# Moving the operands of the f32r matrix products to multiples of 256 bytes

## The chip, the core and the metric

The kernel runs on one NeuronCore of a Trainium2 chip. Five engines work side by side: TensorE (PE, with its weight loads shown apart as PEld), VectorE (DVE), ScalarE (ACT), GpSimd (POOL) and SyncE (SP, which only issues DMAs here). The metric is device time in microseconds (us) of one execution; the three runs of the kernel before have a median of 734.86 us (734.58 to 734.96).

On-chip memory (SBUF) has 128 partitions. A tile lies in all of them at the same start address, counted in bytes along the partition. This text gives such an address modulo 512 ("at 192" means that the address leaves 192 when divided by 512).

## The reference

Two attention steps are followed by a gated feed-forward layer, for 8 batches of 576 tokens, 8 heads of 64:

```
def sm_attn(qq, kk, vv):
    s = scale * np.matmul(qq, kk.transpose(0, 1, 3, 2))
    ...
    return np.matmul(a, vv)
p_packed = sm_attn(p, k, v)              # 32 packed queries per head
out = sm_attn(q, p_packed, p_packed)     # 576 queries against 32 packed keys
...
g = x @ w_gate                            # x: 4608 x 512, w_gate, w_val: 512 x 1536
silu = g * (1.0 / (1.0 + np.exp(-g)))
val = x @ w_val
return (silu * val @ w_out).astype(np.float32)
```

## The kernel before

The weights arrive as 64-bit floats and are converted on the chip (lines 192 to 201). For each batch the kernel multiplies the packed values with the two input weight matrices first, which gives a matrix M for the batch (`m_mm`, line 575, products at line 267), and then multiplies the attention weights of the 576 queries (`a2`) with M: this gives the gate and the value (`gv_chunk`, line 619, products at line 633). ScalarE takes the silu, VectorE multiplies, and the result h is multiplied with w_out (`out_mm`, line 650, products at line 652). d_ff is worked through in 12 chunks of 128.

The large products are made in f32r, a faster float32 form of lower precision. To keep the precision each operand is split into a high and a low word (`mh` and `ml` for M, `a2h` and `a2l`, `hh` and `hl`, `wo_h` and `wo_l`), and three products replace one: low by high, high by low, high by high. Of each product one operand is stationary (loaded into the array by an LDWEIGHTS) and one is moving (streamed through it). At line 633 M is stationary (128 columns, 512 bytes of a partition) and a2 is moving (256 or 320 columns); at line 652 h is stationary and w_out is moving (512 columns). Batch 0 makes its products at lines 787 and 828, some of them in plain float32, where one product shows as two MATMUL rows.

The order of the instructions of every engine is written out by hand: `PROGRAM` for batch 0, the tables `FIRST` and `LATER` for the others. Nothing in it is chosen by a planner from addresses or sizes.

Tiles are laid one after another in SBUF in the order in which their names first occur, so a longer tile shifts all that follow it. Three tiles of the kernel before are longer than what they hold: `pp` by `PAD` = 120 elements (480 bytes), `r2` by 52 elements (208 bytes), and `t4` by 48 elements (192 bytes); only the part that is used is ever read. The starts that result, in the built program:

| tile | used as | start modulo 512, before |
|---|---|---|
| w0 to w5 | moving, line 267 | 192 |
| wo_h, wo_l, wo_f | moving, lines 652 and 828 | 192 |
| a2h, a2l | moving, lines 633 and 787 | 192; its second half 448 |
| a2f | moving, line 787 | 160 (a 32-byte multiple) and 416 |
| mh | stationary, line 633 | 0 |
| ml | stationary, line 633 | 448 |
| hh, hl | stationary, line 652 | 448 |
| ppt | stationary, line 267 | 384 |
| k_t, q_t, v_t, st | DMA targets | 192 |

The a2 tile has two halves of 576 elements (2304 bytes), one for each half of the contraction, and a product starts in it at element 0, 256 or 320. So its moving operand starts at 192 as often as at 448. The slices of M and h start at multiples of 512 bytes from their tile's start.

Of the kernel before, what the change touches and what calls it, by code (L numbers as in the profile page):

```python
# [10 lines left out]
F32 = mybir.dt.float32  # L11
# [12 lines left out]
P = 128  # L24
NPAR, NHP = 2, 4
NFC = DF // P
# [9 lines left out]
F64_HI_LEAST = float(np.array(897 << 20, np.int32).view(np.float32))  # L36
F64_HI_MOST = float(np.array(0x47EFFFFF, np.int32).view(np.float32))
SPLIT = 5
PAD = 120
LOW_WORD = -(2.0**-51) * 15 / 16  # L40

PROGRAM = """
# [90 lines left out]
def tile_pack_attention_swiglu(ctx: ExitStack, tc: tile.TileContext, qT, kT, v, vq, pT, wgv, wout, out):  # L133
# [4 lines left out]
    const = ctx.enter_context(tc.tile_pool(name="const", bufs=1))  # L138
    pool = ctx.enter_context(tc.tile_pool(name="pool", bufs=1))
# [9 lines left out]
    minus_two = const.tile([P, 1], F32, name="minus_two")  # L149
    nc.gpsimd.memset(minus_two, -2.0)  # L150

    w_t = [const.tile([P, NHP, 2, 2 * P], F32, name=f"w{k}") for k in range(NFC // 2)]

    def run_all(*gens):
        for g in gens:
# [202 lines left out]
    def s1_scale(b):  # L358
        pp = pool.tile([P, NPAR * D + PAD], F32, tag="pp", bufs=1, name="pp")[:, : NPAR * D].rearrange(
            "p (r d) -> p r d", r=NPAR  # L360
        )
        nc.vector.tensor_tensor(
            pp,
            pps[b][0][:, : NPAR * D].rearrange("p (r d) -> p r d", r=NPAR),
            st1[b][2][:, 2].unsqueeze(2).broadcast_to([P, NPAR, D]),
            op=ALU.mult,
        )
        pps[b].append(pp)
# [236 lines left out]
    t4 = {}  # L605
# [113 lines left out]
    with tc.manual_schedule(engines={mybir.EngineType.PE}):  # L719
# [12 lines left out]
            return rows, [ps_acc.tile([P, 512], F32, tag="acc", name="acc") for _ in range(4)]  # L732

        def t4_of(b):
            t4[b // 2] = pool.tile([P, NFC * P + 48], F32, tag="t4", bufs=1, name="t4")[:, : NFC * P].rearrange(
                "p (f t) -> p f t", f=NFC
            )

        with tc.manual_schedule(
            engines={mybir.EngineType.DVE, mybir.EngineType.Activation, mybir.EngineType.SP}  # L740
# [19 lines left out]
            def narrow(_):  # L760
                wide[0] = False
                t4_of(0)
                for x, y in zip((rows, accs), accs_of(0)):
                    x.extend(y)
# [123 lines left out]
            for word in PROGRAM.split():  # L888
                name = word[: word.index(":") + 1] if ":" in word else word.rstrip("0123456789")
# [14 lines left out]
        def batch(b, behind):  # L904
            if not b % 2:
                t4_of(b)
# [114 lines left out]
```

## Time and profile before

| | |
|---|---|
| median of 3 runs | 734.86 us (734.58 to 734.96) |
| the profiled execution | 734.87 us |
| its span, first to last instruction | 733.1 us |
| TensorE busy / weight loads busy | 723.9 us (99%) / 590.4 us (81%) |
| VectorE busy / ScalarE busy | 454.2 us (62%) / 373.7 us (51%) |
| granted TensorE clock | 1.000 |
| share of TensorE in the chain that ended last | 96% |

The profile shows a MATMUL with its time from entering the array to its modelled end, so neighbours overlap. The pace of a stream of products is read from the distance of their starts. The "busy" time of a group counts overlapping time once. The chain of work that ended last follows, from the last instruction back, what each instruction was waiting for; its shares say where a saved microsecond would count.

### The profile page before, as it was taken

Reading aid. Unit: us, or ns where it says so; the run is one execution under the profiler, and the core shown is the slowest. Engines: PE = TensorE matmul, PEld = TensorE weight load, DVE = VectorE, ACT = ScalarE, POOL = GpSimd, SP = SyncE. Lnnn points to the kernel's source line nnn. Section 1 sums busy time; section 2 is a strip of 40 time slices with the busy share of each in tenths; the row PEclk is TensorE's granted clock in tenths of the full one; section 3 lists DMA queues with packets and bytes.
Section 4 is the critical chain, followed back from the end, with each engine's and each line's share of the span. In section 5 each row is a group of like instructions: output and inputs, shape, how many; then the busy total and the mean of one; then the engine's idle time right before and its main releaser. Section 6 shows DMA issues by size and latency. Waiting matters only on the chain.

```text
span 733.1 us, 15099 instructions
## 1 busy us (share of the span) xinstructions
PE 723.9 (99%) x6242; PEld 590.4 (81%) x6242; DVE 454.2 (62%) x1009; ACT 373.7 (51%) x668; POOL 2.0 (0%) x13
## 2 busy tenths in 40 slices
PE   8899999999999999999999999999999999999997
PEld 4655667888888888888888888888888888888886
DVE  4999779665755557664764646665574655744333
ACT  3779737754635445553563535654453535533331
POOL 0000000000000000000000000000000000000000
PEclk9999999999999999999999999999999999999999
DMA  9697482310112201302112011102001000010001
GB/s 344 269 346 276 140 315 95 111 73 2 65 58 85 74 1 66 126 4 73 66 48 93 21 57 65 43 19 73 1 2 72 4 2 1 1 59 1 1 1 72
DMA packets 20004, 59.15 MB, mean 81 GB/s; under 512 B 5984, under 2 KB 7008, under 8 KB 17376
## 3 DMA queue, kind: packets, MB, share of 16 engines
q1 hardware_dynamic: 19792, 58.12, 21.9%
q8 instruction: 49, 0.80, 0.5%
q14 instruction: 19, 0.16, 0.1%
q10 hardware_dynamic: 144, 0.07, 0.0%
HBM read 48.69 MB, written 9.49 MB: 79 GB/s over the span
## 4 chain that ended last, share of the span: by engine, by line
PE 96%; DVE 1%; issue 0%; DVEq 0%
PE gv L633 36%; PE acc L652 34%; PE aux L267 7%; PE gv L787 6%; PE acc L828 5%; PE aux L652 4%; PE gv_aux L482 1%; PE gv_aux L398 1%; PE gv_aux L267 1%; DVE w L200 0%; PE acc L726 0%; PE aux L343 0%; DVE w L201 0%; PE aux L324 0%; DVE ot L180 0%; PE aux L398 0%
## 5 line engine op out<-in xcount | busy, mean ns | idle before, releaser
L640 ACT ACTIVATE sg<-gv 128x256 f32<-128x256 f32 (+1 forms) x168 | 69.0, 411 | 175.3 <-PE gv L633 161.6
L644 DVE TENSOR_TENSOR hf<-gv,sg 128x256 f32<-128x256 f32 x168 | 71.0, 422 | 129.8 <-PE gv L633 118.5
L633 PE MATMUL gv<-a2h,ml 128*128 128x256 f32 (+1 forms) x672 | 143.5, 295 | 0.0
L633 PE MATMUL gv<-a2l,mh 128*128 128x256 f32 (+1 forms) x672 | 143.4, 295 | 0.0
L633 PE MATMUL gv<-a2h,mh 128*128 128x256 f32 (+1 forms) x672 | 143.4, 295 | 0.0
L652 PE MATMUL acc<-wo_h,hl 128*128 128x512 f32 x344 | 139.8, 406 | 0.0
L652 PE MATMUL acc<-wo_l,hh 128*128 128x512 f32 x344 | 135.5, 394 | 0.0
L652 PE MATMUL acc<-wo_h,hh 128*128 128x512 f32 x344 | 135.5, 394 | 0.0
L633 PEld LDWEIGHTS gv<-a2h,ml 128*128 128x128 f32 x672 | 116.4, 189 | 15.3 <-ACT sg L803 0.4
L178 ACT CAST hh<-hf 128x256 fp32r<-128x256 f32 x168 | 67.7, 403 | 101.9 <-DVE hf L644 101.8
L633 PEld LDWEIGHTS gv<-a2l,mh 128*128 128x128 f32 x672 | 107.8, 189 | 0.0
L633 PEld LDWEIGHTS gv<-a2h,mh 128*128 128x128 f32 x672 | 107.6, 188 | 0.0
L614 DVE TENSOR_TENSOR hl<-hf,hh 128x256 fp32r<-128x256 f32 x168 | 69.8, 416 | 46.4 <-ACT hh L178 46.3
L652 PEld LDWEIGHTS acc<-wo_h,hl 128*128 128x128 f32 x344 | 64.5, 188 | 28.0 <-issue 19.2
L652 PEld LDWEIGHTS acc<-wo_h,hh 128*128 128x128 f32 x344 | 64.6, 188 | 14.6
L652 PEld LDWEIGHTS acc<-wo_l,hh 128*128 128x128 f32 x344 | 64.6, 188 | 8.3 <-issue 0.2
L571 DVE TENSOR_TENSOR ml<-aux,mh 128x512 fp32r<-128x512 f32 x92 | 58.9, 682 | 5.4 <-ACT mh L597 5.4
L267 PE MATMUL aux<-w,ppt 64*32 64x512 f32 (+1 forms) x784 | 52.1, 588 | 0.9 <-DVE w L201 0.9
L597 ACT CAST mh<-aux 128x512 fp32r<-128x512 f32 x92 | 49.4, 590 | 5.6 <-PE aux L267 1.2
L640 ACT ACT_TABLE_LOAD x30 | 38.5, 1283 | 13.6 <-PE gv L633 9.8
L828 PE MATMUL acc<-wo_f,h 128*128 128x512 f32 x80 | 37.8, 602 | 0.0
L828 PEld LDWEIGHTS acc<-wo_f,h 128*128 128x128 f32 x80 | 14.2, 189 | 16.7 <-issue 16.2
(153 smaller groups left out, 754.3 us busy)
## 6 DMA issues: line engine op xcount, KB each, us to landing
st<-in_wgv SPq DMA_DIRECT2D x12, 1024.0 KB, 7.6
k_t<-in_kT SPq DMA_DIRECT2D x16, 576.0 KB, 4.9
q_t<-in_qT SPq DMA_DIRECT2D x16, 576.0 KB, 4.9
out<-ot SPq DMA_DIRECT2D x36, 256.0 KB, 2.1
v_t<-in_vq SPq DMA_DIRECT2D x6, 1280.0 KB, 5.7
st<-in_wout SPq DMA_DIRECT2D x6, 1024.0 KB, 6.8
v_t<-in_v SPq DMA_DIRECT2D x2, 1024.0 KB, 8.7
p_t<-in_pT SPq DMA_DIRECT2D x7, 64.0 KB, 2.4
```

What stands on the lines that cost most here:

```text
L178: e.copy(dst, src)
L267: nc.tensor.matmul(outs[par][32 * hp : 32 * hp + 32], lhs(r, hp), rhs(r, hp), start=True, stop=True)
L398: nc.tensor.matmul(pss[par][NP * j : NP * j + NP, i * SQ : (i + 1) * SQ], p_t[r, 2 * g + i, :], k_t[r, j // 2, 2 * g + i, j % 2 * SQ : j % ...
L571: pin(nc.vector.tensor_tensor(*lows.pop(0), op=ALU.subtract))
L597: nc.scalar.copy(m[0][at], src)
L614: low = lo.tensor_tensor(hl, src, hh.bitcast(F32), op=ALU.subtract)
L633: nc.tensor.matmul(pg[:, :n], m_[:, g, f, s * P : (s + 1) * P], a_[:, g, off : off + n], start=(i == 0), stop=(i == 5),)
L640: nc.scalar.activation(sg[:, :n], pgs[0][:, :n], AF.Silu)
L644: nc.vector.tensor_tensor(hf, pgs[1][:, o : o + 256], sg[:, o : o + 256], op=ALU.mult)
L652: nc.tensor.matmul(acc[:, :], h_[:, c : c + P], w_[fc // 2][:, fc % 2], start=(fc == 0 and i == 0), stop=(fc == NFC - 1 and i == 2),)
L787: nc.tensor.matmul(held[i][s][:, :n], m_[:, g, f, s * P : (s + 1) * P], a_[:, g, off : off + n], start=(j == 0), stop=(j == len(todo) - 1),)
L828: nc.tensor.matmul(accs[2 * is_b + c], half(i)[:, c * P : c * P + P], wos[fc // 2][:, fc % 2], start=(fc == 0), stop=(fc == NFC - 1),)
```

## The change

Three tile lengths are altered, and nothing else: `PAD` falls from 120 to 40 elements, the last of the six weight tiles (`w5`) gets 80 elements (320 bytes) that are never read, and `t4` loses its 48.

```diff
-PAD = 120
+PAD = 40
...
-    w_t = [const.tile([P, NHP, 2, 2 * P], F32, name=f"w{k}") for k in range(NFC // 2)]
+    w_t = [
+        const.tile([P, NHP * 4 * P + (80 if k == NFC // 2 - 1 else 0)], F32, name=f"w{k}")[:, : NHP * 4 * P].rearrange(
+            "p (h f n) -> p h f n", h=NHP, f=2
+        )
+        for k in range(NFC // 2)
+    ]
...
-            t4[b // 2] = pool.tile([P, NFC * P + 48], F32, tag="t4", bufs=1, name="t4")[:, : NFC * P].rearrange(
-                "p (f t) -> p f t", f=NFC
-            )
+            t4[b // 2] = pool.tile([P, NFC, P], F32, tag="t4", bufs=1, name="t4")
```

The instructions, their order on each engine and their semaphore waits are the same in both built programs; only addresses differ. The starts of the built program with the change:

| tile | before | with the change |
|---|---|---|
| w0 to w5 | 192 | 192 |
| wo_h, wo_l, wo_f | 192 | 0 |
| a2h, a2l | 192 and 448 | 0 and 256 |
| a2f | 160 and 416 | 224 and 480 |
| mh | 0 | 0 |
| ml | 448 | 256 |
| hh, hl | 448 | 256 |
| ppt | 384 | 384 |
| k_t, q_t, v_t, st | 192 | 0 |

## The prediction

> **What bounds the kernel now.** The first view is the list of cores, for the clock, and then the page's busy shares and its chain of waits. One core, full clock, TensorE busy in 99% of the span; the chain that ended last is TensorE for 96%, and 70% of it is two lines.
>
> ```profile
> core 0: 733.1 us, clock 1.000
> PE 723.9 (99%) x6242; PEld 590.4 (81%) x6242; DVE 454.2 (62%) x1009; ACT 373.7 (51%) x668; POOL 2.0 (0%) x13
> PE 96%; DVE 1%; issue 0%; DVEq 0%
> PE gv L633 36%; PE acc L652 34%; PE aux L267 7%; PE gv L787 6%; PE acc L828 5%; PE aux L652 4%; PE gv_aux L482 1%; PE gv_aux L398 1%; PE gv_aux L267 1%; DVE w L200 0%; PE acc L726 0%; PE aux L343 0%; DVE w L201 0%; PE aux L324 0%; DVE ot L180 0%; PE aux L398 0%
> ```
>
> So the pace of the f32r products of lines 633 and 652 decides, and with them line 652's part into aux and the f32r share of batch 0 (line 787). The counts come from the groups of TensorE by shape:
>
> ```profile
> L652 PE MATMUL acc<-wo_h,hl 128*128 128x512 f32 x344 | 139.8, 406 | 0.0
> L633 PE MATMUL gv<-a2h,ml 128*128 128x320 f32 x336 | 76.5, 309 | 0.0
> L633 PE MATMUL gv<-a2l,mh 128*128 128x320 f32 x336 | 76.3, 308 | 0.0
> L633 PE MATMUL gv<-a2h,mh 128*128 128x320 f32 x336 | 76.2, 308 | 0.0
> L633 PE MATMUL gv<-a2h,mh 128*128 128x256 f32 x336 | 67.1, 281 | 0.0
> L633 PE MATMUL gv<-a2h,ml 128*128 128x256 f32 x336 | 67.1, 281 | 0.0
> L633 PE MATMUL gv<-a2l,mh 128*128 128x256 f32 x336 | 67.0, 281 | 0.0
> L652 PE MATMUL aux<-wo_h,hl 128*128 128x512 f32 x48 | 18.7, 390 | 0.0
> ```
>
> Line 633 has 6 x 336 = 2016 products, line 652 has 3 x 344 = 1032 into acc and 3 x 48 = 144 into aux. The printed mean (309 ns) includes a modelled tail, so the pace is read from the timeline, as the distance of starts (first column the start in us):
>
> ```profile
> 399.85 0.40 PE L633 MATMUL gv<-a2h,ml 128*128 128x256 f32 x2
> 401.27 0.39 PE L652 MATMUL acc<-wo_h,hl 128*128 128x512 f32 x1
> 402.65 0.45 PE L633 MATMUL gv<-a2h,ml 128*128 128x320 f32 x2
> 404.40 0.39 PE L652 MATMUL acc<-wo_h,hl 128*128 128x512 f32 x1
> ...
> 720.99 0.39 PE L652 MATMUL aux<-wo_h,hl 128*128 128x512 f32 x1
> 724.39 0.39 PE L652 MATMUL aux<-wo_h,hl 128*128 128x512 f32 x1
> ```
>
> Between the first two rows stand 12 products of 256 columns: 1.42 us / 12 = 118.3 ns each. Between the second and third stand six of 512: 1.38 / 6 = 230 ns. Between the third and fourth twelve of 320: 1.75 / 12 = 145.8 ns. In the long row of products at the end, 15 products of 512 columns take 3.40 us: 226.7 ns each.
>
> Is that slower than it could be? Plain float32 shows it. In the chain by pieces, batch 0 has plain products (one passes twice through the array, so a row of x4 is two products):
>
> ```profile
> 36.62 1.72 PE acc L828 x4
> 44.78 2.15 PE gv L787 x8
> 49.44 1.73 PE gv L787 x8
> ```
>
> One pass takes 1.72 / 4 = 430 ns for 512 columns, 2.15 / 8 = 268.8 for 320, 1.73 / 8 = 216.3 for 256. A plain pass reads its moving operand at half the rate. Half of a plain pass is 215, 134.4 and 108.1 ns; an f32r product takes 226.7 (230 in a group of six), 145.8 and 118.3. The **excess** of f32r is 11.7 (15.0), 11.4 and 10.2 ns. That is what placement could be worth, if anything on TensorE depends on it.
>
> **The change part by part.**
>
> *Addresses only.* No instruction, wait or DMA is added, removed or moved, so every term is a change of pace at an unchanged count. Three questions are left: whether the distance between the stationary and the moving operand counts, whether the absolute start counts, and what happens to the engines beside TensorE.
>
> *The distance.* Everything but M's high words, the weights w and ppt moves by the same 320 bytes modulo 512. For line 652 h stands 448 - 192 = 256 from w_out before, and 256 - 0 = 256 after: unchanged for 1176 products. For line 633 the low words stand 0 or 256 from a2 (448 against 448 or 192), and still do. Only the high words change: 0 against 192 or 448, a distance of 320 or 64, becomes 0 against 0 or 256. That is exactly the pair of distances that the low words have now. So the price stands in the groups above: what `a2h,ml` takes, against what `a2l,mh` and `a2h,mh` take. At 320 columns 76.5 against 76.3 and 76.2 us; at 256 columns 67.1 against 67.0 and 67.1. If the high words took on the low words' whole time, that would be 0.2 + 0.3 + 0.1 + 0 = 0.6 us more over 1344 products, 0.4 ns each. From below: the low words' products also come first in each chunk, so the 0.6 can be the handover from the stage before, and the term is 0. I take 0, since a distance that counted would show in the 256-column rows too, and these are level within 0.1 us in 67.
>
> *The absolute start, stationary.* High words at 0 and low words at 448 are both in the trace, at the same pace as just shown. ml moves from 448 to 256, another multiple of 64, and h with it. I take 0.
>
> *The absolute start, moving.* Here the trace has no case: every f32r moving operand starts at 192 or 448, which is 192 modulo 256, and goes to a multiple of 256. Plain products do show two other starts: at line 787 a2f begins at 160 or 416, a multiple of 32 only, and its 256 columns take 216.3 ns a pass, where 512 columns from 192 take 430; both come to 0.84 ns per column. But they read at half the rate, so they bound nothing for f32r. What speaks for a price of 0 is the form of the excess. If starting off a multiple of 256 broke the stream at every such boundary, the excess would grow with the columns: 512 columns would pay twice what 256 pay. It is 10.2, 11.4 and 11.7 ns, nearly the same for each product, as a cost of changing the stationary operand would be. The 512-column product crosses eight boundaries of 256 bytes with its 2048 bytes and pays no more than the 320-column one, which crosses five. Bounds: from below, the whole excess gone; from above, as much again on the products where both operands start at the same place. Both ends are priced as rivals below. I take 0, as the level rows are nearer to it than to either end.
>
> The Trainium skill ("TensorE: Matmul & The Clock Gate", Part 2, step 1) says that the array has two independent read ports, and that loading the next weights does not steal read bandwidth from the running product. By that rule the excess is not the load's doing, and where the moving operand lies would be the next suspect; by it the low end of the range gains weight. The rows make the excess a cost per product, so I give it little.
>
> *VectorE and ScalarE.* Their operands move too, but both are off the chain (62% and 51% busy). What they wait for is TensorE:
>
> ```profile
> ACT sg L640 <- PE gv L633: 161.6, 121, 4.5
> DVE hf L644 <- PE gv L633: 118.5, 105, 2.4
> ACT w L197 <- DMA st<-in_wgv: 3.3, 3, 1.5
> ACT wo_f L197 <- DMA st<-in_wout: 2.3, 1, 2.3
> ```
>
> ScalarE stands idle for 161.6 us ahead of the silu, in 121 pieces of 1.3 us on average. A few per cent on instructions of 0.4 us disappears in that. If this cover were gone, each of the 168 chunks would pass its own delay on to TensorE: 1% of 0.41 us is 4 ns, times 168 is 0.7 us. I take 0.
>
> *The loads.* k_t, q_t, v_t and the weights' staging tiles begin at 0 instead of 192. Only the last two rows above show a wait for loads of weights: 5.6 us in four waits. A load that is 2% quicker or slower lands 0.15 us earlier or later (2% of 7.6):
>
> ```profile
> st<-in_wgv SPq DMA_DIRECT2D x12, 1024.0 KB, 7.6
> ```
>
> Four such waits make 0.6 us either way at most; I take 0. The Trainium skill ("DMA: Bandwidth & Descriptors", How a descriptor splits into AXI transactions) says that a descriptor that does not start on 256 bytes pays one transaction more. By it, as an estimate, a row of 8192 bytes would take 32 instead of 33, and the sum would be up to 0.9 us lower.
>
> *Sum.* 734.87 us of the profiled execution (733.1 of span and 1.8 around it) + 0 (distance, 0 to 0.6) + 0 (start) + 0 (loads, -0.6 to 0.6) = **734.9 us**. The profiled execution lies 0.01 us from the median of the three runs, so nothing is to be converted.
>
> **The rivals.**
>
> *Faster, a little (F1).* The long row of products at the end runs at 226.7 ns, the groups of six at 230. If these 3.3 ns were a matter of how the operands lie, and line 633 paid the same, the change could give them back on 160 groups of six (960 products) and 2016 products: 2976 x 3.3 = 9.8 us, which gives 725.1. For it: the difference is there at an even clock. Against it: the operands of both rows lie at the same places modulo 512 (192 and 448), so what differs is the neighbourhood, not the placement.
>
> *Faster, all of it (F2).* A start at a multiple of 256 removes the excess: 960 x 15.0 + 216 x 11.7 + 1008 x 11.4 + 1008 x 10.2 = 14.4 + 2.5 + 11.5 + 10.3 us, and some 2 for batch 0's 192 f32r products, in all 40.8, which gives 694.1. For it: the plain rows have no excess. Against it: the excess per product, not per column.
>
> *Slower (S).* One place, line 633: with the change half of the products of the high words, 672, have their stationary operand and their moving one both at 0 modulo 512. If the weight load and the stream meet in the same part of the memory and each product pays the excess once more (10.8 on average), that costs 672 x 10.8 = 7.3 us: 742.2. It decides as soon as a shared start costs over 2.2 ns, since 672 x 2.2 is the 1.5 us that can be told apart. Against it: half of the low words' products share a start of 448 already and are no slower. For it: 448 is not 0, and no f32r product of the trace has both at 0.
>
> That the change doesn't move what it names can be excluded: the starts in the built program are those listed.
>
> **How the numbers follow.** No change 0.55; F1 0.15; F2 0.05; S 0.17; a small shift that I don't name (start-up loads, a wait that tips over) 0.08, of which 0.05 faster and 0.03 slower. A measurement of this kernel can tell about 0.2%, 1.5 us, from no change. So faster is 0.15 + 0.05 + 0.05 = 0.25, same 0.55, slower 0.17 + 0.03 = 0.20. The predicted time is that of no change, 734.9. Its own range is 733.7 to 736.1 (the bounds of distance and loads). The range for 8 in 10 reaches above to S at 742.2, with rounding 743; below it holds the small shifts and four fifths of F1, to 727, and leaves F1's full size and F2 (0.20) outside.
>
> **What would show it.** In the profile of the changed kernel: twelve products of 256 columns in 1.42 us, six of 512 in 1.38, twelve of 320 in 1.75, and 226.7 ns in the long row at the end, would show each step right. If `a2l,mh` and `a2h,mh` take more than `a2h,ml`, the distance counts after all (S). If line 652 changes its pace, with its distance unchanged, the absolute start counts and the argument from the even excess was wrong. If TensorE's lines stand still and the time moves by over 1.5 us, it is the start-up: the waits for the staged weights would show it.

## The result, and the profile after

The changed kernel takes **736.33 us** (median, 735.45 to 738.08) where the kernel before, beside it, takes 735.0 us: a ratio of 1.0016, with a 95% interval of 1.0009 to 1.0023. That is 1.3 us more, a loss that is real but just under the 0.2% taken as the line. The profiled execution took 736.54 us, 1.7 us more than that of before (734.87).

The page of the changed kernel, busy time of each engine, and its list of cores:

```profile
core 0: 734.8 us, clock 1.000
PE 725.3 (99%) x6242; PEld 592.3 (81%) x6242; DVE 454.6 (62%) x1009; ACT 373.9 (51%) x668; POOL 2.0 (0%) x13
```

The span grew by 1.7 us (733.1 to 734.8) at the same clock and the same counts, TensorE's busy time by 1.4 (723.9 to 725.3), and the other engines' by 0.4 at most. So the loss is in the pace of TensorE. Its groups by shape, of the changed kernel (line 633 is now 638, line 652 is 657; the last columns are busy us, mean ns and idle us before):

```profile
L657 PE MATMUL acc<-wo_h,hl 128*128 128x512 f32 x344 | 140.5, 408 | 0.0
L657 PE MATMUL acc<-wo_l,hh 128*128 128x512 f32 x344 | 135.7, 395 | 0.0
L657 PE MATMUL acc<-wo_h,hh 128*128 128x512 f32 x344 | 134.6, 391 | 0.0
L638 PE MATMUL gv<-a2h,mh 128*128 128x320 f32 x336 | 76.5, 309 | 0.0
L638 PE MATMUL gv<-a2h,ml 128*128 128x320 f32 x336 | 76.4, 309 | 0.0
L638 PE MATMUL gv<-a2l,mh 128*128 128x320 f32 x336 | 76.4, 308 | 0.0
L638 PE MATMUL gv<-a2l,mh 128*128 128x256 f32 x336 | 67.7, 283 | 0.0
L638 PE MATMUL gv<-a2h,mh 128*128 128x256 f32 x336 | 67.5, 282 | 0.0
L638 PE MATMUL gv<-a2h,ml 128*128 128x256 f32 x336 | 67.2, 282 | 0.0
```

At 256 columns the two groups of the high words rose by 0.7 and 0.4 us (from 67.0 and 67.1), the low words' by 0.1. The 320-column groups moved by 0.3 at most and in both directions. Line 657 stands at 140.5, 135.7 and 134.6 us. Its first group of before, shown ahead, took 139.8; these are the other two of before:

```profile
L652 PE MATMUL acc<-wo_l,hh 128*128 128x512 f32 x344 | 135.5, 394 | 0.0
L652 PE MATMUL acc<-wo_h,hh 128*128 128x512 f32 x344 | 135.5, 394 | 0.0
```

The sum is the same. The timeline of the changed kernel gives the pace (first column the start in us):

```profile
400.26 0.40 PE L638 MATMUL gv<-a2h,ml 128*128 128x256 f32 x2
...
401.69 0.40 PE L657 MATMUL acc<-wo_h,hl 128*128 128x512 f32 x1
...
403.08 0.45 PE L638 MATMUL gv<-a2h,ml 128*128 128x320 f32 x2
...
404.83 0.39 PE L657 MATMUL acc<-wo_h,hl 128*128 128x512 f32 x1
```

Twelve products of 256 columns take 1.43 us, where one such group took 1.42 before; the six of 512 take 1.39 (1.38), the twelve of 320 take 1.75 (1.75). One group with two decimals can't carry 1.3 us in 84 groups, so the starts were taken of all 84 groups of twelve in the two traces, in ns, and averaged. Products 1 and 2 of a group have a low word of M loaded, 3 to 6 a high one, 7 and 8 a low one, 9 to 12 a high one; the time is from a product's start to that of the next, and the twelfth hands over to 512 columns:

```
product       1      2      3      4      5      6      7      8      9     10     11     12
before    115.3  118.2  117.9  118.2  117.6  119.4  120.0  117.5  118.2  117.5  117.5  164.7
changed   114.4  119.2  120.0  120.0  120.0  120.0  120.0  120.0  120.0  120.0  120.0  164.6
```

A group of twelve grew by 16.2 ns, and 84 groups give 1.4 us. The starts of the 320-column products give another 0.2 us, and those of line 657 nothing. This is the loss: 1.6 of the 1.7 us in the span. The upper line also shows what the prediction didn't see. **Products 6 and 7 took 119.4 and 120.0 ns before already.** They are the two behind which a low word follows. A product's weights are loaded while the product ahead of it runs, as the weight loads of the kernel before show in the same stage (PEld, first column the start):

```profile
399.97 0.31 PEld L633 LDWEIGHTS gv<-a2l,mh 128*128 128x128 f32 x2
400.21 0.31 PEld L633 LDWEIGHTS gv<-a2h,mh 128*128 128x128 f32 x2
```

The first load of `a2l,mh` begins at 399.97, while the second `a2h,ml` product still runs; the first product of its own begins at 400.08. So a load can slow the product before its own. In the kernel before, products 6 and 7, which ran beside a low-word load (distance 0 or 256 from the streamed a2), took 119.4 to 120, those beside a high-word load (distance 64 or 320) about 118; product 1, also beside a low-word load, took 115.3 and doesn't fit. With the change every load stands at 0 or 256, and nearly every product takes 120.

This sorting is a reading of these two lines and not a rule. In two experiments below, with w_out alone moved and with the high words put back, the low words' loads stand at 0 or 256 as well, and products 6 and 7 took 115.3 and 118.5 ns in the one, 115.1 and 116.8 in the other. What a product takes depends on more than the load beside it.

The start-up did not decide. The waits for staged weights went from 5.6 us to 4.8:

```profile
ACT sg L645 <- PE gv L638: 164.0, 123, 4.5
DVE hf L649 <- PE gv L638: 120.1, 105, 2.5
ACT w L202 <- DMA st<-in_wgv: 2.7, 2, 1.8
ACT wo_f L202 <- DMA st<-in_wout: 2.1, 1, 2.1
```

ScalarE and VectorE wait 2.4 and 1.6 us more for TensorE than before: they follow it.

### The profile page after: what moved, and what is told of

It is laid out like the page before. It is cut to its first block, busy times and chain, and to the rows that moved or that the text cites. A ratio compares the mean times of both kernels' runs of the same rounds, so it can differ in the third digit from the quotient of the medians.

```text
span 734.8 us, 15099 instructions
## 1 busy us (share of the span) xinstructions
PE 725.3 (99%) x6242; PEld 592.3 (81%) x6242; DVE 454.6 (62%) x1009; ACT 373.9 (51%) x668; POOL 2.0 (0%) x13
## 4 chain that ended last, share of the span: by engine, by line
PE 96%; DVE 1%; issue 0%; DVEq 0%
PE gv L638 36%; PE acc L657 34%; PE aux L272 7%; PE gv L790 6%; PE acc L831 5%; PE aux L657 4%; PE gv_aux L487 1%; PE gv_aux L403 1%; PE gv_aux L272 1%; DVE w L205 0%; PE acc L731 0%; PE aux L348 0%; DVE w L206 0%; PE aux L329 0%; DVE ot L185 0%; PE aux L403 0%
## 5 line engine op out<-in xcount | busy, mean ns | idle before, releaser
L649 DVE TENSOR_TENSOR hf<-gv,sg 128x256 f32<-128x256 f32 x168 | 71.0, 423 | 131.5 <-PE gv L638 120.1
L657 PE MATMUL acc<-wo_h,hl 128*128 128x512 f32 x344 | 140.5, 408 | 0.0
L657 PE MATMUL acc<-wo_l,hh 128*128 128x512 f32 x344 | 135.7, 395 | 0.0
L657 PE MATMUL acc<-wo_h,hh 128*128 128x512 f32 x344 | 134.6, 391 | 0.0
L831 PEld LDWEIGHTS acc<-wo_f,h 128*128 128x128 f32 x80 | 14.2, 189 | 16.6 <-issue 16.2
```

Of the source, the lines that this page charges most:

```text
L649: nc.vector.tensor_tensor(hf, pgs[1][:, o : o + 256], sg[:, o : o + 256], op=ALU.mult)
L657: nc.tensor.matmul(acc[:, :], h_[:, c : c + P], w_[fc // 2][:, fc % 2], start=(fc == 0 and i == 0), stop=(fc == NFC - 1 and i == 2),)
L831: nc.tensor.matmul(accs[2 * is_b + c], half(i)[:, c * P : c * P + P], wos[fc // 2][:, fc % 2], start=(fc == 0), stop=(fc == NFC - 1),)
```

## The experiments

Three theories stood at the start. **D**: the distance, modulo 256 bytes, between the weights that are being loaded and the operand that is streamed sets the pace. **A**: the absolute start of an operand does. **N**: neither; the 1.3 us come from elsewhere. All ratios are to the kernel before, run beside the experiment. Medians of the kernel before beside them were 734.9 to 735.1 us.

**The pace alone.** A kernel of f32r products only, 24 for each distance from 0 (`dist_a`) to 480 (`dist_p`) in steps of 32 bytes, with the streamed operand at 0 (`mz`) and at 192 (`mq`), for 256, 320 and 512 columns:

```diff
+        for f in (n256, n320, n512):
+            for mv, start in ((mz, 0), (mq, 192)):
+                for d in range(16):
+                    at = (start + 32 * d) % 512 // 4
+                    for j in range(COUNT):
+                        f(to, mv, at + j % 4 * P)
```

> Leaves out the whole computation: f32r products alone, 24 in each group, with 16 distances (start of the stationary operand minus start of the moving one, 0 to 480 in steps of 32 bytes, modulo 512; a letter a to p each) for a moving operand at 0 (mz) and at 192 (mq), at 256, 320 and 512 columns. Theory D (the distance between the weights being loaded and the operand being streamed decides): at 256 columns distances 0 and 256 (a, i) take 120.0 ns a product and 64 and 320 (c, k) about 118, the same for mz and mq; 320 and 512 columns differ by under 1 ns between the distances. Rival A (the moving operand's absolute start decides): mz takes 120 at every distance, mq 118. Rival N (neither; the 2 ns come from the neighbouring instructions in the kernel): all 32 groups of 256 columns alike within 0.5 ns.

Its timeline, a row for each 24 products:

```profile
21.52 3.03 PE L66 MATMUL dist_a<-mz,st 128*128 128x256 f32 x24
24.39 3.00 PE L66 MATMUL dist_b<-mz,st 128*128 128x256 f32 x24
27.23 2.99 PE L66 MATMUL dist_c<-mz,st 128*128 128x256 f32 x24
30.06 2.98 PE L66 MATMUL dist_d<-mz,st 128*128 128x256 f32 x24
...
44.26 3.03 PE L66 MATMUL dist_i<-mz,st 128*128 128x256 f32 x24
47.13 3.00 PE L66 MATMUL dist_j<-mz,st 128*128 128x256 f32 x24
...
66.98 3.03 PE L66 MATMUL dist_a<-mq,st 128*128 128x256 f32 x24
69.85 3.00 PE L66 MATMUL dist_b<-mq,st 128*128 128x256 f32 x24
...
112.44 3.68 PE L66 MATMUL dist_a<-mz,st 128*128 128x320 f32 x24
115.96 3.68 PE L66 MATMUL dist_b<-mz,st 128*128 128x320 f32 x24
...
230.56 5.75 PE L66 MATMUL dist_b<-mz,st 128*128 128x512 f32 x24
236.15 5.76 PE L66 MATMUL dist_c<-mz,st 128*128 128x512 f32 x24
...
269.67 5.61 PE L66 MATMUL dist_i<-mz,st 128*128 128x512 f32 x24
275.12 5.75 PE L66 MATMUL dist_j<-mz,st 128*128 128x512 f32 x24
```

From start to start, 256 columns at distance 0 take 2.87 / 24 = 119.6 ns, at 64 take 2.83 / 24 = 117.9, and at 256 again 119.6; with the streamed operand at 192 instead of 0, distance 0 takes 119.6 too. At 320 columns it is 3.52 / 24 = 146.7 ns; at 512 columns distance 32 takes 5.59 / 24 = 232.9, and 256 takes 227.1. Without the first four of each 24, where the step to the new distance lies, in ns:

```
distance modulo 256       0     32     64     96    128    160    192    224
256 columns           120.0  118.3  117.7  117.3  118.5  120.1  117.8  117.8
512 columns           226.7  233.4  233.5  234.3  233.6  233.6  228.9  233.3
320 columns           146.6 to 146.7 at every distance
```

D stands for long rows of equal products: the pace has a period of 256 bytes in the distance, and the two starts of the streamed operand, 0 and 192, differ by 0.3 ns at most at 256 columns and 0.5 at 512. A and N fall. The 2.3 ns between distances 64 and 0 are about what the change took on. The expectation of under 1 ns between the distances held at 320 columns and missed at 512: there 0 is the *fastest*, by some 7 ns against most others.

**The change without its step on a2.** `t4` keeps its 48 elements, so a2, M and h stay where they were; only w_out and the staging tiles move to 0, and h stands at 192 (modulo 256) from w_out:

```diff
-            t4[b // 2] = pool.tile([P, NFC, P], F32, tag="t4", bufs=1, name="t4")
+            t4[b // 2] = pool.tile([P, NFC * P + 48], F32, tag="t4", bufs=1, name="t4")[:, : NFC * P].rearrange(
```

> One part alone: w_out, h0 and the staging tiles at 0 as with the change, a2, M and h as before (distance of h from w_out 448 instead of 256). D: line 633 keeps 118.3 ns at 256 columns, so the time is that of before within 0.1% (ratio 0.999 to 1.001) unless distance 448 has a price of its own at 512 columns. A: line 652's moving operand is at 0 now, and line 633's is not: line 633 stays at 118.3, line 652 may move by up to 2 ns (2.4 us, ratio 1.003).

Measured: 735.62 us, ratio 1.0009 (1.0000 to 1.0017). The long row of 512-column products went from 227.9 to 229.7 ns on average, where the table has 226.7 and 228.9. On 144 products that is 0.3 us. From start to start the f32r products of 256 columns (batch 0's included, here and below) are 0.5 us quicker than before, not slower, and those of 320 columns 0.8 us slower. So what the change did to line 638 is not in this part of it.

**The step on a2 alone.** The kernel before, without the 48 elements of `t4`; a2 goes to 0 and 256, ml and h to 256, w_out stays at 192, so h stands at 64 from it:

```diff
-            t4[b // 2] = pool.tile([P, NFC * P + 48], F32, tag="t4", bufs=1, name="t4")[:, : NFC * P].rearrange(
-                "p (f t) -> p f t", f=NFC
-            )
+            t4[b // 2] = pool.tile([P, NFC, P], F32, tag="t4", bufs=1, name="t4")
```

> The other part alone: a2 at 0 and 256, low words of M and h at 256, w_out stays at 192 (distance of h from w_out 64). D and A: the high words' loads take 120 ns at 256 columns and line 633 is about 1.4 us longer than before (ratio 1.002); D: with h 64 from w_out line 652 is level or up to 1 us faster. N: no difference from before.

Measured: 738.47 us, ratio 1.0055 (1.0042 to 1.0068), profiled 738.14 us. The expectation missed that half: distance 64 costs line 652 something. From start to start its products into acc take 1.4 us more than before, the long row into aux 0.8 (233.3 ns instead of 227.9), and the products of 256 columns 1.05: together 3.3 us, as much as the span grew (733.1 to 736.4).

**The weights at 64 from what is streamed, but for the long row.** The kernel before, with two tile lengths changed so that ml and the words of h that go into acc start at 0. The words of h that go into aux, in the long row, are tiles of their own; they lie behind `sg`, whose 16 elements more bring them back to 448, at 0 (modulo 256) from w_out. So the text below, which takes every load of line 652 to be at 64, doesn't hold for the 144 products into aux:

```diff
-        x = pool.tile([P, NJ + 6, 2, H], F32, tag="x1", bufs=1, name="x1")[:, :NJ]
+        x = pool.tile([P, NJ + 5, 2, H], F32, tag="x1", bufs=1, name="x1")[:, :NJ]
...
-        sg = pool.tile([P, NB], F32, tag="sg", bufs=1, name="sg")
+        sg = pool.tile([P, NB + 16], F32, tag="sg", bufs=1, name="sg")
```

> Before, with low words of M and h moved by 64 bytes to 0, so that every load of lines 633 and 652 is 64 or 320 bytes from the operand streamed beside it. D: the low words' loads fall from 120 to 118 ns at 256 columns, some 0.3 to 0.7 us less than before (ratio 0.9992), more if 512 columns profit too. A: as before, since no moving operand moves. N: as before.

Measured: 734.12 us, ratio 0.9987 (0.9978 to 0.9996), profiled 733.01. Its 256-column groups of TensorE:

```profile
L633 PE MATMUL gv<-a2h,ml 128*128 128x256 f32 x336 | 66.1, 278 | 0.0
L633 PE MATMUL gv<-a2h,mh 128*128 128x256 f32 x336 | 65.5, 276 | 0.0
L633 PE MATMUL gv<-a2l,mh 128*128 128x256 f32 x336 | 65.5, 276 | 0.0
```

The products of 256 columns gain 3.9 us from start to start, line 652 loses 1.8 into acc, and the 320-column products lose 0.6. The sign is D's, but the size isn't: after the first of a group the products run at 113.4 to 114.3 ns, and D's table has 117.7. There is a quicker state that the distance alone doesn't give. The long row stays at 227.7 ns, as its distance of 0 lets one expect from the table (226.7), where the experiment before, with the long row at 64, had 233.3 (table 233.5).

**Which layout gives the quick state.** The f32r products of one stage in the kernel's order (twelve of 256 columns, six of 512, twelve of 320, six of 512), eight stages for each layout; the three numbers of a layout are the distances of M's high words, its low words and h:

```diff
+LAYOUTS = (
+    (64, 0, 0), (0, 0, 0), (64, 64, 64), (64, 64, 0), (0, 0, 64), (96, 96, 0), (128, 128, 0), (160, 160, 0), (192, 192, 0),
+    (32, 32, 0), (224, 224, 0),
+)
```

> Leaves out the whole computation: the f32r products of lines 633 and 652 alone, in the kernel's order (12 of 256 columns, 6 of 512, 12 of 320, 6 of 512), 8 stages for each of 11 layouts. A layout is the distance of the high words of M, its low ones, and of h: a 64,0,0 (as before), b 0,0,0 (as with the change), c 64,64,64, d 64,64,0, e 0,0,64, f 96,96,0, g 128,128,0, h 160,160,0, i 192,192,0, j 32,32,0, k 224,224,0. Theory D (each load has the price of its own distance, as the long rows of equal products showed it): 256 columns take 118.4 in a, 120 in b, e and h, 117.7 in c, d, i and k, 117.3 in f; c loses at 512 columns against d. Theory H (what a load costs also depends on what the ones before it left over, as in the run with all loads at 64): c and d take about 113.5 at 256 columns, a 118, b 120, and 512 columns in groups of six are nearly level between distance 0 and 64. Rival R (other engines' work in the kernel made the difference): all layouts alike within 0.5 ns.

The first product of each layout's stages, by tile (minimum, median and maximum ns, then the first and the last start in us):

```profile
L83 PE MATMUL lay_a<-ah,ml x64: 277/294/309, 24.2 to 69.6; 128*128 128x256 f32 x32, 128*128 128x320 f32 x32
L83 PE MATMUL lay_b<-ah,ml x64: 277/294/309, 71.7 to 117.3; 128*128 128x256 f32 x32, 128*128 128x320 f32 x32
L83 PE MATMUL lay_c<-ah,ml x64: 276/294/310, 119.4 to 164.7; 128*128 128x256 f32 x32, 128*128 128x320 f32 x32
L83 PE MATMUL lay_d<-ah,ml x64: 276/292/310, 166.8 to 212.1; 128*128 128x256 f32 x32, 128*128 128x320 f32 x32
```

From the first start of one layout to that of the next are eight stages. `a`, the layout of before, takes 47.5 / 8 = 5.94 us; `b`, that of the change, 47.7 / 8 = 5.96. With more digits it is 5.940 and 5.960, and 20 ns in 84 stages (7 batches of 12 chunks) are 1.7 us: the growth of the span. So the products alone, in their order, hold the whole loss. `c`, with all three at 64, is in the quick state (113.8 ns, 5.920 us once it has settled). `d` has the same M, and h at 0, and is not (117.8, 5.933). What M's products take depends on the h products between them, so the theory that a product's own distance is all falls here. H, which expected the quick state in `d` too, was wrong there, and the 256-column products of `e` (0, 0, 64) took 117.9 ns where D expected 120.

**The same in the kernel.** Both words of M at 64 from a2, h at 0 from w_out:

```diff
-PAD = 40
+PAD = 104
...
-(80 if k == NFC // 2 - 1 else 0)
+(16 if k == NFC // 2 - 1 else 0)
...
-        sg = pool.tile([P, NB], F32, tag="sg", bufs=1, name="sg")
+        sg = pool.tile([P, NB + 16], F32, tag="sg", bufs=1, name="sg")
```

(`t4` keeps its 48 and `x1` is four rows shorter.)

> Before, with both words of M at 64 (modulo 256) from a2, and h still at 0 from w_out (w_out at 256, h at 0). H: 256 columns fall from 118.2 to about 113.5 ns as in the run with all loads at 64 (-3.9 us), and 512 columns stay as before instead of losing 1.8 us: 731.2, ratio 0.995. D: 117.7 at 256 columns, -0.7 us, ratio 0.999. A: as before.

Measured: 733.65 us, ratio 0.9984 (0.9975 to 0.9993). The gain is there and smaller than the quick state would make it: 256 columns stay at 118 ns, as in layout `d`, and 1.6 us come from the 512-column products into acc (229.6 ns instead of 231.4, handovers that wait left out); the 320-column products take 0.8 us more. Why the products into acc are quicker, at an unchanged distance of 0, is open.

**More layouts**, the same kernel of stages with 16 others:

```diff
+    (64, 0, 192), (192, 192, 192), (192, 192, 64), (64, 64, 192), (96, 96, 64), (224, 224, 64), (224, 224, 192), (96, 96, 192),
+    (192, 64, 0), (64, 192, 0), (192, 0, 0), (0, 64, 0), (0, 0, 192), (192, 64, 64), (64, 192, 64), (64, 0, 0),
```

> Leaves out the whole computation: the same stages as in the run before with layouts, 16 other layouts (high words, low words, h): a 64,0,192 (as in the run with w_out alone moved), b 192,192,192, c 192,192,64, d 64,64,192, e 96,96,64, f 224,224,64, g 224,224,192, h 96,96,192, i 192,64,0, j 64,192,0, k 192,0,0, l 0,64,0, m 0,0,192, n 192,64,64, o 64,192,64, p 64,0,0 (again as before). If the stage's time belongs to the layout alone (H), p repeats 5.940 us within 0.003 although it stands elsewhere, a is within 0.005 of it (its kernel was 0.2 us longer in the profile, over 84 stages), and stages with h at 64 start their 256-column group in the quick state of 113.5 ns only if M is at 64 too. If the state came from the place in the program (rival), p differs by over 0.01. For the best layout: any stage under 5.915 us would be worth over 2 us in the kernel.

By tile, the same columns as above:

```profile
L83 PE MATMUL lay_d<-ah,ml x64: 276/295/310, 165.7 to 210.7; 128*128 128x256 f32 x32, 128*128 128x320 f32 x32
L83 PE MATMUL lay_e<-ah,ml x64: 278/295/310, 212.9 to 258.4; 128*128 128x256 f32 x32, 128*128 128x320 f32 x32
...
L83 PE MATMUL lay_j<-ah,ml x64: 276/295/309, 450.2 to 495.3; 128*128 128x256 f32 x32, 128*128 128x320 f32 x32
L83 PE MATMUL lay_k<-ah,ml x64: 277/294/310, 497.4 to 542.8; 128*128 128x256 f32 x32, 128*128 128x320 f32 x32
```

`d` (64, 64, 192) and `j` (64, 192, 0) take 47.2 / 8 = 5.90 us a stage; with more digits 5.893 and 5.900, the quickest two. The layout of before, at the end this time (`p`), takes 5.940 us again, so the numbers belong to the layouts and not to their place in the run. The expectation for `a` missed: the layout with w_out alone moved takes 5.953 us, 13 ns more than that of before, which would be 1.1 us in 84 stages, and in its kernel the span grew by 0.2. Four of the 16 layouts run their 256 columns at 113.7 to 114.7 ns: (64, 64, 192), (64, 192, 0), (192, 64, 64) and (64, 192, 64), at 5.893 to 5.914 us a stage. All of them have a word of M at 64 and the other at 64 or 192, and none of the layouts with a word of M at 0 is below 5.940. The rule expected of h (the quick state only with both of M's words and h at 64) fell: h at 192 and at 0 give it too, each with another M. (192, 64, 0) has the same starts as `j` with M's words exchanged, and runs at 117 ns: no simple rule is left.

**The cause, undone.** The change, with only the high words' distance put back, by 16 elements less in `r2` and 16 more in `t4`; low words, h and w_out keep the distances of the change:

```diff
-            pool.tile([P, 6 * NPAR * NBK + 52], F32, tag="r2", bufs=1, name="r2")[:, : 6 * NPAR * NBK].rearrange(
+            pool.tile([P, 6 * NPAR * NBK + 36], F32, tag="r2", bufs=1, name="r2")[:, : 6 * NPAR * NBK].rearrange(
...
-            t4[b // 2] = pool.tile([P, NFC, P], F32, tag="t4", bufs=1, name="t4")
+            t4[b // 2] = pool.tile([P, NFC * P + 16], F32, tag="t4", bufs=1, name="t4")[:, : NFC * P].rearrange(
```

> The change with one thing undone: the high words of M stand 192 (modulo 256) from a2 instead of 0; w_out, h, a2 and the low words stay where the change put them. If the change's loss is the high words' distance, the loss goes: the stage of this layout took 5.940 us, like that of before, so the time is that of before within 0.1% (1.2 to 1.7 us under the change). If it is the absolute starts (multiples of 256) or the other engines' operands, it stays 1.2 us over before, ratio 1.0016.

Measured: 734.48 us, ratio 0.9990 (0.9981 to 1.0000), profiled 734.72. Its 256-column groups:

```profile
L638 PE MATMUL gv<-a2h,ml 128*128 128x256 f32 x336 | 67.0, 281 | 0.0
L638 PE MATMUL gv<-a2l,mh 128*128 128x256 f32 x336 | 66.9, 281 | 0.0
L638 PE MATMUL gv<-a2h,mh 128*128 128x256 f32 x336 | 66.6, 279 | 0.0
```

67.7 and 67.5 us fell to 66.9 and 66.6, and the loss is gone. With layouts `a` and `b` above, which differ in this distance alone and by the same 1.7 us, the high words' distance is shown to be its cause.

**The two quickest layouts in the kernel.** (64, 64, 192), then (64, 192, 0), both from the change:

```diff
-PAD = 40
+PAD = 88
...
-(80 if k == NFC // 2 - 1 else 0)
+(32 if k == NFC // 2 - 1 else 0)
...
-        sg = pool.tile([P, NB], F32, tag="sg", bufs=1, name="sg")
+        sg = pool.tile([P, NB + 16], F32, tag="sg", bufs=1, name="sg")
```

> For a faster version: both words of M at 64 from a2, h at 192 from w_out, the quickest stage of the 27 (5.893 against 5.940 us). If a kernel's gain is the stage's over its 84 stages, it is 3.9 us under before: 731.0, ratio 0.9946. If the quick state is lost among the kernel's other products, it is between 0 and 2 us under.

Measured: 735.27 us, ratio 1.0003 (0.9995 to 1.0012). The stage promised 84 x (5.893 - 5.940) = -3.9 us; nothing came. The 256-column products run at about 118 ns in all 84 groups. Other products of the kernel, such as those that make M, stand between many of the stages, but 37 of the 84 groups follow a whole stage in the order of the stage kernel with no other product between, and they run at 117.7 to 117.9 ns as well. In the stage kernel this layout was at its 5.893 us from its first stage on. So other products just ahead of a group are not what keeps it out of the quick state; what does is open.

```diff
-PAD = 40
+PAD = 72
...
-(80 if k == NFC // 2 - 1 else 0)
+(48 if k == NFC // 2 - 1 else 0)
...
-        sg = pool.tile([P, NB], F32, tag="sg", bufs=1, name="sg")
+        sg = pool.tile([P, NB + 48], F32, tag="sg", bufs=1, name="sg")
```

(In both `t4` keeps its 48, and `x1` is shorter by three and by four rows.)

> For a faster version: high words at 64, low ones at 192 from a2, h at 0 from w_out (stage 5.900 us). By the stage 3.4 us under before: 731.5, ratio 0.9954; if the quick state is lost among the other products, between 0 and 2 us under.

Measured: **733.06 us, ratio 0.9971 (0.9960 to 0.9983)**, profiled 732.69: quicker than both kernels. Its 256-column groups:

```profile
L638 PE MATMUL gv<-a2l,mh 128*128 128x256 f32 x336 | 66.4, 279 | 0.0
L638 PE MATMUL gv<-a2h,ml 128*128 128x256 f32 x336 | 66.0, 277 | 0.0
L638 PE MATMUL gv<-a2h,mh 128*128 128x256 f32 x336 | 65.8, 277 | 0.0
```

From start to start they gain 2.8 us over before, and the 320-column products lose 0.7; the later products of a group run at 113.3 to 113.5 ns. The span fell by 2.2 us (733.1 to 730.9), where the stage promised 3.4.

## Why the prediction was right, and where it wasn't

The time came out 1.4 us above the 734.9 predicted, 0.2 us above the top of the forecast's own range (736.1). The measured ratio of 1.0016 still lies in the 0.2% that was called no change. That the forecast came out so is luck in part: the loss is real, its term had been put at 0, and it stayed under the line of 1.5 us by 0.2. Step by step:

- **What bounds the kernel** held: the other engines' busy time stayed, and the pace of the f32r products is 1.6 us of the 1.7 in the span.
- **The distance, taken as 0 with 0.6 at most,** is the step that failed. It measured 1.4 us at 256 columns. The pair of distances was found rightly (0 and 256, as the low words have them), but its price was read off the wrong rows: from `a2h,ml` against the two groups of `mh`. A load runs beside the product before its own, so each group was a mixture. In twelve products of before, three have a low-word load beside them: 1, 6 and 7. Products 6 and 7 took 119.4 and 120.0 ns, and stood one in `a2h,mh` and one in `a2h,ml`; product 1 took only 115.3, for a reason that no run here shows. So the level groups (67.0 to 67.1 us) were no evidence. Sorted by the load beside them, the rows of before give 120.0 - 117.5 = 2.5 ns between products 7 and 8; on the 672 products of 256 columns that run beside a high-word load that is 1.7 us. This hint was there to be read. That it came so near the 1.4 is worth less than it looks, since the same two products took other times in other layouts with the same loads. The sign that the prediction had named came: in the changed kernel the groups of `mh` took 67.7 and 67.5 us and `a2h,ml` 67.2.
- **"A distance that counted would show in the 256-column rows too"** named the right rows, but products and not groups had to be compared. At 320 columns the pace in long equal rows is 146.6 to 146.7 ns at all distances.
- **The absolute start, 0 for both operands,** held: in the rows of equal products the streamed operand at 0 or 192 makes no difference beyond 0.5 ns.
- **The unchanged distance of line 652** held: its products into acc sum to the same time, and the long row takes 227.8 ns on average where it took 227.9. What a price there would be, the experiment with a2 alone shows: 2.2 us.
- **The excess as a cost per product.** At distance 0 it is 11.9, 12.2 and 11.7 ns for 256, 320 and 512 columns, so it doesn't grow with the columns crossed, and no start removes it. At distance 64 it is 9.6, 12.2 and 18.5: that the place of the operands has no part in it was wrong. That it is a cost of changing the stationary operand is not shown, as no run has f32r products without a load each.
- **The rule of the Trainium skill** ("TensorE: Matmul & The Clock Gate", Part 2, step 1), that loading the next weights doesn't steal read bandwidth from the running product, would let one expect a pace that doesn't care where the weights lie. The measurement differs: with the streamed operand unchanged, moving the loaded weights alone moves the pace from 117.3 to 120.1 ns at 256 columns and from 226.7 to 234.3 at 512. Whether read bandwidth is what is lost, no run shows.
- **VectorE, ScalarE and the loads, 0**: held for the time. The median landing of a staged block went from 7.6 to 6.1 us. With the staging tile still at 192 it was 6.7 and 6.6 us in the experiments with a2 alone and with the weights at 64; with it at 0, as in the change, it was 5.7 and 6.5 with w_out alone and with the high words put back. A part of the placement in this is neither shown nor excluded. The waits for the staged weights fell by 0.8 us in all, a little over the 0.6 allowed, a wait of 0.7 us for v_t went and one of 0.2 for k_t came; with 1.6 us of the span's 1.7 in the products, next to nothing of it reached the time.
- **The range.** Its upper end, 736.1, is the sum of the terms' bounds. Its lower end of 733.7 is not: the distance could only add, so the terms give 734.3.
- **The rivals.** F1 and F2 fell: no f32r product gets rid of its excess by starting at a multiple of 256. S had the right place and the right kind of dependence (where the load lies against the stream), with the wrong price: 1.4 us on its 672 products are 2 ns a product instead of 10.8. The objection to it ("half of the low words' products share a start of 448 already and are no slower") was the misreading above. The point from which S was to decide, 2.2 ns, is nearly what was measured. S also asked for a shared start at 0; the runs show that any distance of 0 modulo 256 does it.

## What to carry to other kernels

A weight load runs beside the product before its own: look at products by their place in the sequence, and by the load that runs beside them, before calling two operands level by the means of their groups. In long rows of f32r products with a load each, the distance modulo 256 bytes between loaded weights and streamed operand was worth 2 to 3% of a product, with different best values for 256 and 512 columns, and padding a tile by a few elements sets it. In the kernel's mixed order the table isn't enough. Try layouts in the kernel itself: the same products alone foretold the loss of this change well, and one of two gains not at all.

## What was not expected of the hardware

- **The pace of f32r depends on a distance of addresses.** In rows of equal products: period 256 bytes; 117.3 to 120.1 ns at 256 columns, 226.7 to 234.3 at 512, no effect at 320. At 256 columns 0 is among the worst distances, at 512 it is the best. In the kernel the 320-column products do react: they take 0.6 to 0.8 us more than before in four of the experiments. Why the best is opposite, and why 320 columns react there and not in equal rows, is open.
- **A state that is carried on.** The same 256-column products at the same distances take 113.8 or 117.8 ns, by where h lies in the products between them (layouts `c` and `d` of the first kernel of stages). In the kernel the quick state was seen in two layouts, and not in a third, (64, 64, 192), that had it in the stage alone, not even in the 37 groups that follow a whole stage with no other product between. Its rule is open.
